# Bound rows through the accumulator, and two kinds of scaling moved to GpSimd, in a two-layer attention and feed-forward kernel

## The chip, the core and the metric

The kernel runs on one core of a Trainium2 chip. The core has five engines with queues of their own: TensorE (PE; its weight loads are shown as PEld), VectorE (DVE), ScalarE (ACT), GpSimd (POOL) and SyncE (SP), which here only issues DMAs. Each engine works through its instructions in the order in which the program was written, and they meet at semaphores. The metric is the device time of one execution in microseconds.

## The reference

The input `A_x` has 2048 tokens of 512 values. Two kinds of layer alternate, A, B, A, B; each adds to its input. A is attention with 32 heads of 16 values and no mask, B is a feed-forward net with 1376 hidden values:

```python
qkv = (layernorm(x) @ wqkv)                      # 32 heads of 16
p = softmax(q @ k^T * 16 ** -0.5)                # 2048 x 2048 for each head
x = x + (p @ v) @ wo
x = x + gelu(layernorm(layernorm(x)) @ w1 + b1) @ w2 + b2
```

Layers 1 and 3 in the kernel's names are the two pairs of A and B. Inputs and output are bfloat16.

## The kernel before, in words

**Segments and tiles.** Attention works in segments: one head group of four heads (`hg`, eight of them), and one unit of queries (512 tokens; the last unit of layer 3 is split into two of 256). A segment has 64 score tiles of 128 keys by 512 queries (16 key blocks times four heads); its scores are transposed, keys on partitions. The first unit of each layer is cut in two parts by keys (`nparts == 2`), since part of the keys is not there yet: in layer 1, key blocks 0 to 3 and then 4 to 15, in layer 3, 0 to 11 and then 12 to 15. So there are 88 segments: 16 in parts and 24 whole ones in layer 1, 16 in parts, 16 whole ones and 16 of half width in layer 3.

**Exponentials without a maximum.** Each head has 32 columns in the stored queries and keys: 16 values, and in column 16 a 1 on the key's side and a bound on the query's side, minus the norm of the query; `scl` multiplies it by the largest norm among the keys of the part. So the score product itself subtracts a bound that no score exceeds. The two key parts of a segment have different bounds; when their sums are merged, the first part is multiplied by the exponential of the difference of the two bounds, which `job_segend` reads from row 16 of each head's 32 rows of the scaled query `QT`.

**Two engines take exponentials.** ScalarE turns groups of two or three score tiles in PSUM into bfloat16 with `Exp` (L1374). For key blocks 3, 6, 9, 12 and 15 (`DK`, 20 of a segment's 64 tiles) VectorE may do it instead: L1466 turns a score into the bits of a bfloat16 that approximates its exponential, and L1497 makes three shifted copies. The four are multiplied by four versions of the values (V and three scaled ones, `vs`, made on GpSimd by L1157 and for whole segments read back from memory). So a tile on VectorE needs four products with the values (L1563), one on ScalarE needs one.

**Accumulation.** L1563 accumulates the products in bank 6 of PSUM (`ACCB`), 17 rows in each of four column tiles: 16 values, and the sum of the weights by a column of ones. At a segment's end `job_segend` transposes the bank to `accT` (L1593). Segments in parts also transpose their `QT` into a slot of `xn` (L1602) and take from it row 16: part 0 keeps it as `rowA` (L1608), part 1 takes the difference (L1618), ScalarE its exponential (L1620), and four instructions on GpSimd merge the parts (L1621 to L1624). Then the sums are divided out (L1626, L1635).

**Queries.** `flow_q` brings a segment's queries by a transposing DMA to one of two slots of `qraw`. `job_qt` waits for one of three slots of `QT` and for `scl`, and scales them (L1132). The slot of `QT` is given back in `job_segend`, after the transposes.

**Normalisation.** `ln_group` makes mean and variance (L846, L847) and, on GpSimd, the reciprocal deviation (L854, L855). `ln_apply` (L859) applies them to one tile of 128 tokens in a slot of `xn`, three in number. `job_qkv_tile` does that ahead of the projections to queries, keys and values (in layer 1 twice for tiles 4 to 15, first for keys and values, later for queries; in layer 3 once), `job_yt` ahead of the feed-forward net. A transposing DMA on SP follows (L893, L1696). The first four tiles of layer 1 have a way of their own (`job_first_tile`), and the last 256 tokens another (`tail_tile`).

**The order of the work.** A planner in the program (`Sched`) simulates the five engines with a duration for each instruction and writes each engine's queue in the order of the simulated time, by priority among what is ready. `take_d` gives a tile to VectorE when its simulated queue is short enough and a bank and a buffer are free; everything else goes to ScalarE. A duration, an instruction or a slot that changes can thus change the order of all the rest. In a second pass (`refill`) it puts products with zeros (L1295, L1297, L1299) into gaps of TensorE. The fields of `I(...)` are the function, the resources read and written, the planner's duration, and two more; `"fast"` marks VectorE instructions that the planner lengthens, by the last field of a GpSimd instruction, where both run at once.

Of the kernel before, what the change touches and what calls it, by code (L numbers as in the profile page):

```python
# [8 lines left out]
BF16 = mybir.dt.bfloat16  # L9
# [5 lines left out]
ALU = mybir.AluOpType  # L15
# [252 lines left out]
def I(fn, reads=(), writes=(), dur=0.3, same_ok=(), lat=None):  # L268
    return (fn, tuple(reads), tuple(writes), tuple(same_ok), dur, lat)
# [231 lines left out]
ACCB = 6  # L501
# [10 lines left out]
class Builder:  # L512
# [45 lines left out]
    def alloc(self, es):  # L558
        nc = self.nc
        S, NT, NC, NFC = self.S, self.NT, self.NC, self.NFC  # L560
        t = lambda name, shape, dt: es.enter_context(nc.sbuf_tensor(name, shape, dt))
# [13 lines left out]
        self.sel = t("sel", [32, 128], BF16)  # L575
        self.onesm = t("onesm", [128, 1], F32)
# [107 lines left out]
    def build_startup(self):  # L684
# [46 lines left out]
        def consts():  # L731
# [10 lines left out]
            yield dve(lambda e: e.tensor_copy(out=self.sel[:, :].rearrange("p (h c) -> p h c", c=32)[:, :, 16], in_=self.m4[:, :]), [("m4",)], [("sel",)])  # L742
            self.S_.mark(("consts",))
# [113 lines left out]
    def ln_apply(self, tt, slot, i, dst, dres, prio):  # L857
        c = 4 * slot + i
        return Task("dve", prio, [I(lambda e: e.tensor_scalar(out=dst, in0=self.xres[:, tt, :], scalar1=self.mv[:, c, 0:1], scalar2=self.rs[:, c:c + 1], op0=ALU.subtract, op1=ALU.mult),  # L859
                                    [("x", tt), ("mv", c), ("rs", slot)], [dres], 0.395, (), "fast")])  # L860
# [21 lines left out]
    def job_qkv_tile(self, L, tt, slot, i, left, prio, what):  # L882
        S_ = self.S_
# [3 lines left out]
        yield self.ln_apply(tt, slot, i, xnr, RX, prio)  # L887
# [236 lines left out]
    def job_qt(self, sg, s):  # L1124
        L, part, hg = sg["L"], sg["part"], sg["hg"]
        k = (L // 2) * 2 + part
        q = yield ("get", "qt")
        sg["qslot"] = q
        yield ("keys", [("scl", L, part)])
        W = sg["W"]  # L1130
        src, RS = (self.psbf(self.q0bank)[:, 0:512], ("ps", self.q0bank)) if s is None else (self.qraw[:, s, 0:W], ("qraw", s))
        yield Task("dve", 0.4, [I(lambda e: e.tensor_scalar(out=self.QT[:, q, 0:W], in0=src, scalar1=self.scl[:, k, hg:hg + 1], scalar2=self.qbias[:, 0:1], op0=ALU.mult, op1=ALU.add),  # L1132
                                  [RS, ("scl", k), ("qbias",)], [("qt", q)], 0.16 + 0.24 * W / 512, (), "fast")])
# [380 lines left out]
    def try_pv(self):  # L1514
        S_ = self.S_
        while True:
# [35 lines left out]
            for (s_, j, res, ap, use, sh) in pick:  # L1552
# [3 lines left out]
                sg["first"].add(hp)  # L1556
                for i, kb in enumerate(kbs):
# [28 lines left out]
    def job_segend(self, sg):  # L1586
# [11 lines left out]
        if nparts == 2:  # L1598
            xs = yield ("get", "xn")
            RX = ("xn", xs)  # L1600
            rowT = self.xn[:, xs, :].rearrange("p (b r) -> p b r", r=32)
            yield Task("dve", 1.2, [I(lambda e: e.transpose(self.xn[:, xs, :], self.QT[:, q, :]), [("qt", q)], [RX], 0.68)])  # L1602
# [4 lines left out]
        if nparts == 2 and part == 0:  # L1607
            yield Task("dve", 1.2, [I(lambda e: e.tensor_copy(out=self.rowA[:, hg, :], in_=rowT[:, :, 16]), [RX], [("rowA", hg)], 0.17)])  # L1608
            S_.release("xn", xs)
# [5 lines left out]
        if nparts == 2:  # L1615
            dw = self.dw[:, hg % 2, :]
            RW = ("dw", hg % 2)
            yield Task("dve", 1.2, [I(lambda e: e.tensor_tensor(out=dw, in0=rowT[:, :, 16], in1=self.rowA[:, hg, :], op=ALU.subtract), [RX, ("rowA", hg)], [RW], 0.17)])  # L1618
            S_.release("xn", xs)
# [69 lines left out]
    def job_yt(self, L, tt, slot, i, left, pr):  # L1689
        S_ = self.S_  # L1690
        xr = yield ("get", "xn")
        yield self.ln_apply(tt, slot, i, self.xn[:, xr, :], ("xn", xr), pr - 1)
# [237 lines left out]
```

## Time and profile before

| what | value |
|---|---|
| median of 3 runs | 1602.69 us (1601.01 to 1605.23) |
| profiled execution | 1603.4 us, its span 1601.8 us |
| busy, VectorE | 1473.8 us (92%) |
| busy, ScalarE | 1535.5 us (96%) |
| busy, GpSimd | 207.0 us (13%) |
| L1602, L1132, L859 on VectorE | 32, 88 and 74 instructions |
| segments' ends (L1593) | 88, from 33.9 to 1578.4 us |

Engines are named PE, PEld, DVE, ACT, POOL and SP in the profile; `L1374` is line 1374 of the kernel. A group's row has the line, the engine, the operation, what it writes and reads, the shapes and the count; then busy time in us and the mean of one in ns; then the idle time of its engine just before it, and what ended it. A row of stages has the stretch in us, its length, the busy time and number of instructions for each engine, the granted clock of PE, the busy share of the DMA engines and their GB/s. A row of a timeline has start and duration in us, and in brackets the idle time before and what ended it.

### The profile page before, as it was taken

To read this page: it belongs to the slowest core of one execution; us is meant where nothing else is said; L and a number is where in the kernel's file an instruction comes from. 1 tells how busy PE (TensorE), PEld (TensorE's weight loads), DVE (VectorE), ACT (ScalarE), POOL (GpSimd) and SP (SyncE) were. 2 spreads that over 40 slices of the span, in tenths; PEclk is the share of its full clock that TensorE was granted. 3 is DMA by queue.
4 is the path that set the end of the run, shared out by engine and by line. 5 is a ranking of instruction groups with operands and counts; after the bars stand their busy time and mean duration, and the time that the engine had idled before them with its cause. 6 is when DMAs were issued, how large, how long until landed. Compare 5 with 4: busy or idle time off the path is not lost.

```text
span 1601.8 us, 39236 instructions
## 1 busy us (share of the span) xinstructions
PE 1571.1 (98%) x16532; PEld 481.3 (30%) x16532; DVE 1473.8 (92%) x3323; ACT 1535.5 (96%) x1366; POOL 207.0 (13%) x406
## 2 busy tenths in 40 slices
PE   9999999999999999999999999999999999999998
PEld 3222222222222222222222233222222222344454
DVE  7999999999999899989999899999899989998893
ACT  6999999999999999989999989999999999999995
POOL 4464210000200001001211124300000000000000
PEclk9999999999999999999999999999999999999999
DMA  6671011213321122222822232210101100211100
GB/s 168 122 168 63 22 31 31 53 30 76 84 44 46 36 62 80 56 61 77 138 45 64 58 71 67 60 26 21 31 15 37 31 22 18 40 40 40 41 22 20
DMA packets 212464, 88.79 MB, mean 55 GB/s; under 512 B 183835, under 2 KB 206656, under 8 KB 212288
## 3 DMA queue, kind: packets, MB, share of 16 engines
q1 hardware_dynamic: 212288, 86.29, 24.0%
q8 instruction: 129, 2.11, 0.6%
q14 instruction: 47, 0.39, 0.1%
HBM read 34.65 MB, written 19.48 MB: 34 GB/s over the span
## 4 chain that ended last, share of the span: by engine, by line
PE 49%; ACT 28%; DVE 20%; issue 1%; DMA 1%; POOL 1%; POOLq 0%; DVEq 0%
ACT PT L1374 25%; PE ps L1389 17%; PE ps L1563 14%; DVE dp L1466 7%; DVE dp L1497 5%; PE ps L1747 4%; PE ps L1704 4%; PE ps L916 4%; PE ps L1295 3%; ACT h L1739 2%; PE ps L1299 1%; DVE accT L1593 1%; PE ps L1297 1%; DVE st L846 1%; PE ps L1649 1%
## 5 line engine op out<-in xcount | busy, mean ns | idle before, releaser
L1374 ACT ACTIVATE PT<-ps 128x1024 bf16<-128x1024 f32 (+1 forms) x1283 | 1457.1, 1269 | 36.0 <-PE ps L1389 30.1
L1389 PE MATMUL ps<-QT,KT 32*128 32x512 bf16 (+1 forms) x4608 | 672.5, 358 | 11.5 <-DVE dp L1466 2.2
L1466 DVE TENSOR_SCALAR dp<-ps 128x512 uint16<-128x512 f32 x921 | 618.7, 683 | 56.7 <-PE ps L1389 54.0
L1497 DVE TENSOR_SCALAR dp<-dp 128x1024 uint16<-128x1024 uint16 (+1 forms) x1410 | 533.0, 421 | 7.4 <-PE ps L1563 3.3
L1563 PE MATMUL ps<-PT,V 128*17 128x512 bf16 (+1 forms) x3568 | 468.3, 358 | 0.0
L1563 PE MATMUL ps<-dp,vs 128*17 128x512 bf16 (+1 forms) x3120 | 441.0, 357 | 0.7 <-DVE dp L1497 0.6
L1389 PEld LDWEIGHTS ps<-QT,KT 32*128 32x128 bf16 x4608 | 169.9, 91 | 541.8 <-ACT PT L1374 260.4
L1563 PE MATMUL ps<-dp,V 128*17 128x512 bf16 (+1 forms) x1040 | 214.5, 357 | 2.3 <-DVE accT L1593 2.0
L1297 PE MATMUL ps<-zw 32*128 32x444 bf16 (+2 forms) x714 | 197.6, 325 | 0.0
L1563 PEld LDWEIGHTS ps<-dp,vs 128*17 128x17 bf16 x3120 | 110.9, 88 | 125.1 <-issue 100.9
L1563 PEld LDWEIGHTS ps<-PT,V 128*17 128x17 bf16 x3568 | 112.3, 88 | 105.3 <-issue 94.4
L1299 PE MATMUL ps<-zw 128*32 128x448 bf16 (+23 forms) x1621 | 142.6, 318 | 0.7 <-DVE dp L1466 0.6
L1295 PE MATMUL ps<-zw 128*128 128x448 bf16 (+17 forms) x560 | 130.6, 334 | 4.1 <-DVE dp L1466 2.2
L854 POOL TENSOR_SCALAR rs<-mv 128x4 f32<-128x4 f32 (+2 forms) x19 | 6.6, 347 | 879.1 <-DVE mv L847 877.7
L1704 PE MATMUL ps<-yT,wf 128*128 128x512 bf16 (+3 forms) x396 | 103.5, 360 | 1.0 <-DVE yT L1830 0.5
L916 PE MATMUL ps<-wqkv,xnT 128*128 128x512 bf16 x336 | 93.1, 382 | 1.0 <-DVE h L929 0.5
L1157 POOL TENSOR_SCALAR vs<-V 128x340 bf16<-128x340 bf16 (+2 forms) x72 | 60.5, 841 | 139.7 <-PE ps L1563 121.6
L1295 PEld LDWEIGHTS ps<-zw 128*128 128x128 bf16 x560 | 42.9, 98 | 83.5 <-issue 52.7
L1563 PEld LDWEIGHTS ps<-dp,V 128*17 128x17 bf16 x1040 | 51.3, 88 | 53.1 <-issue 28.5
L1728 DVE TENSOR_SCALAR h<-ps,b1c 128x512 bf16<-128x512 f32 (+2 forms) x88 | 62.3, 708 | 1.8 <-PE ps L1704 1.5
L1593 DVE STREAM_TRANSPOSE accT<-ps 128x512 f32<-128x512 f32 (+1 forms) x88 | 58.1, 660 | 6.1 <-PE ps L1563 4.9
L1299 PEld LDWEIGHTS ps<-zw 128*32 128x32 bf16 x1621 | 52.4, 95 | 24.7 <-DVE dp L1466 5.7
(172 smaller groups left out, 903.0 us busy)
## 6 DMA issues: line engine op xcount, KB each, us to landing
vs<-vs_scr SPq DMA_DIRECT2D x56, 255.0 KB, 2.7
wf<-in_B_w_dram SPq DMA_DIRECT2D x90, 128.0 KB, 2.8
q_scr<-qk SPq DMA_DIRECT2D x22, 256.0 KB, 2.4
k_scr<-qk SPq DMA_DIRECT2D x12, 256.0 KB, 2.3
out_dram<-xres SPq DMA_DIRECT2D x16, 128.0 KB, 1.7
vs_scr<-vs SPq DMA_DIRECT2D x8, 255.0 KB, 3.8
xres<-in_A_x_dram SPq DMA_DIRECT2D x7, 256.0 KB, 3.1
v_scr<-vst SPq DMA_DIRECT2D x12, 136.0 KB, 1.8
```

Of the source, the lines that this page charges most:

```text
L916: yield Task("pe", prio, [I(lambda e, c=c: e.matmul(self.ps[:, b, :], lhsT=xnT[:, c, :], rhs=self.wqkv[:, c, which * 512:which * 512 + 512 ...
L1295: fn = lambda e: e.matmul(self.ps[:, b, 0:w], lhsT=self.zw[:, 0:128], rhs=self.zw[:, 0:w], start=st, stop=st, skip_group_check=True)
L1297: fn = lambda e: e.matmul(self.ps[:, b, 0:w], lhsT=self.zw[32 * p:32 * p + 32, 0:128], rhs=self.zw[32 * p:32 * p + 32, 0:w], start=st, sto ...
L1299: fn = lambda e: e.matmul(self.ps[32 * p:32 * p + 32, b, 0:w], lhsT=self.zw[:, 0:32], rhs=self.zw[:, 0:w], start=st, stop=st, skip_group_c ...
L1374: S_.submit(Task("act", 1e-5 * gi, [I(lambda e, pt=pt, n=n, b0=b0: e.activation(out=self.PT[:, pt:pt + n, :], in_=self.ps[:, b0:b0 + n, :] ...
L1389: return [I(lambda e, kb=kb, i=i: e.matmul(self.ps[:, b, i * W:(i + 1) * W], lhsT=self.KT[32 * hp:32 * hp + 32, hg, kb * 128:(kb + 1) * 12 ...
L1466: self.S_.submit(Task("dve", 0.0, [I(lambda e: e.tensor_scalar(out=self.dp[:, u, w * 512:(w + 1) * 512], in0=self.ps[:, b, :], scalar1=BIT ...
L1497: yield Task("dve", pr, [I(lambda e, k=k, v=v: e.tensor_scalar(out=self.dp[:, v, 0:N], in0=self.dp[:, u, 0:N], scalar1=float(SHIFT[k]), sc ...
L1563: ops.append((nth[j, sh] + 0.1 * i, I(lambda e, hp=hp, v=v, ap=ap[:, i * W:(i + 1) * W], first=first and i == 0, W=W: e.matmul(self.ps[32 ...
L1593: yield Task("dve", 0.3, [I(lambda e: e.transpose(self.accT[:, a, 0:W], self.ps[:, ACCB, 0:W]), [("ps", ACCB)], [RA], 0.17 + 0.535 * W / 5 ...
L1704: yield Task("pe", pr, [I(lambda e, c=c: e.matmul(self.ps[0:M, b, off:off + W], lhsT=self.w1(fc, c), rhs=self.yT[:, c, 0:W], start=(c == 0 ...
L1747: yield Task("pe", pr, [I(lambda e, fc=fc, i=i, b=b: e.matmul(self.ps[:, b, :], lhsT=self.gt(fc, i, W), rhs=self.w2(L, fc), start=(fc == 0 ...
```

## The change

A new constant `rsel` has, for each head of a group, a matrix of 128 x 18 with a single 1: it picks row 16 of the head's 32 rows of `QT` and puts it into row 17 of the head's column tile. For segments in parts, this product opens the accumulation of each head, so the bound row lies beside the sums in `accT` after the transpose, and `QT` is not transposed any more. `rowA` and the difference are read from `accT`. `job_qt` uses GpSimd from the fifth segment on. `ln_apply` uses GpSimd in `job_qkv_tile` for tiles 0 to 11, and in `job_yt` for all but the last four tiles of layer 1. The planner's durations for both on GpSimd are 1.49 us at full width.

```diff
+        self.rsel = t("rsel", [128, 4, 18], BF16)
...
+            yield dve(lambda e: e.memset(self.rsel[:, :, :], 0.0), [], [("rsel",)], 0.1)
+            yield dve(lambda e: e.tensor_copy(out=self.rsel[:, :, 17], in_=self.iogt[:, :]), [("iogt",)], [("rsel",)], 0.1)
...
-    def ln_apply(self, tt, slot, i, dst, dres, prio):
+    def ln_apply(self, tt, slot, i, dst, dres, prio, eng="dve"):
...
-        return Task("dve", prio, [...
-                                    [("x", tt), ("mv", c), ("rs", slot)], [dres], 0.395, (), "fast")])
+        return Task(eng, prio, [...
+                                    [("x", tt), ("mv", c), ("rs", slot)], [dres], 0.395 if eng == "dve" else 1.49, (), "fast" if eng == "dve" else 0.09)])
...
-        yield self.ln_apply(tt, slot, i, xnr, RX, prio)
+        yield self.ln_apply(tt, slot, i, xnr, RX, prio, "dve" if tt >= 12 else "pool")
...
-        yield Task("dve", 0.4, [...
-                                  [RS, ("scl", k), ("qbias",)], [("qt", q)], 0.16 + 0.24 * W / 512, (), "fast")])
+        eng = "dve" if sg["i"] < 4 else "pool"
+        yield Task(eng, 0.4, [...
+                                  [RS, ("scl", k), ("qbias",)], [("qt", q)], 0.16 + 0.24 * W / 512 if eng == "dve" else 0.21 + 1.28 * W / 512, (), "fast" if eng == "dve" else 0.09)])
...
+                if first and sg["nparts"] == 2:
+                    first = False
+                    ops.append((nth[j, sh] - 0.1, I(lambda e, hp=hp, q=q: e.matmul(self.ps[32 * hp:32 * hp + 18, ACCB, :], lhsT=self.rsel[:, hp, :], rhs=self.QT[:, q, :], start=True, stop=False, skip_group_check=True, tile_position=(0, 32 * hp)),
+                                                     [("rsel",), ("qt", q)], [("ps", ACCB)], W / 2400.0, [("ps", ACCB)], ("col", hp))))
...
-        if nparts == 2:
-            xs = yield ("get", "xn")
-            RX = ("xn", xs)
-            rowT = self.xn[:, xs, :].rearrange("p (b r) -> p b r", r=32)
-            yield Task("dve", 1.2, [I(lambda e: e.transpose(self.xn[:, xs, :], self.QT[:, q, :]), [("qt", q)], [RX], 0.68)])
...
-            yield Task("dve", 1.2, [I(lambda e: e.tensor_copy(out=self.rowA[:, hg, :], in_=rowT[:, :, 16]), [RX], [("rowA", hg)], 0.17)])
-            S_.release("xn", xs)
+            yield Task("dve", 1.2, [I(lambda e: e.tensor_copy(out=self.rowA[:, hg, :], in_=T[:, :, 17]), [RA], [("rowA", hg)], 0.17)])
...
-            yield Task("dve", 1.2, [I(lambda e: e.tensor_tensor(out=dw, in0=rowT[:, :, 16], in1=self.rowA[:, hg, :], op=ALU.subtract), [RX, ("rowA", hg)], [RW], 0.17)])
-            S_.release("xn", xs)
+            yield Task("dve", 1.2, [I(lambda e: e.tensor_tensor(out=dw, in0=T[:, :, 17], in1=self.rowA[:, hg, :], op=ALU.subtract), [RA, ("rowA", hg)], [RW], 0.17)])
...
-        yield self.ln_apply(tt, slot, i, self.xn[:, xr, :], ("xn", xr), pr - 1)
+        yield self.ln_apply(tt, slot, i, self.xn[:, xr, :], ("xn", xr), pr - 1, "dve" if L == 1 and tt >= 12 else "pool")
```

More of the change, by code (lines that the diff above doesn't have):

```diff
@@ L855, in ln_group @@
         yield Task("pool", prio, [I(lambda e: e.tensor_tensor(out=rs, in0=rs, in1=self.cneg[:, 0:n], op=ALU.pow), [R, ("cneg",)], [R], 0.45 + 0.15 * n)])
-    def ln_apply(self, tt, slot, i, dst, dres, prio):
+    def ln_apply(self, tt, slot, i, dst, dres, prio, eng="dve"):
         c = 4 * slot + i
-        return Task("dve", prio, [I(lambda e: e.tensor_scalar(out=dst, in0=self.xres[:, tt, :], scalar1=self.mv[:, c, 0:1], scalar2=self.rs[:, c:c + 1], op0=ALU.subtract, op1=ALU.mult),
-                                    [("x", tt), ("mv", c), ("rs", slot)], [dres], 0.395, (), "fast")])
+        return Task(eng, prio, [I(lambda e: e.tensor_scalar(out=dst, in0=self.xres[:, tt, :], scalar1=self.mv[:, c, 0:1], scalar2=self.rs[:, c:c + 1], op0=ALU.subtract, op1=ALU.mult),
+                                    [("x", tt), ("mv", c), ("rs", slot)], [dres], 0.395 if eng == "dve" else 1.49, (), "fast" if eng == "dve" else 0.09)])
     def dma(self, fn, reads, writes, prio, dur=0.08, lat=None):
@@ L1131, in job_qt @@
         src, RS = (self.psbf(self.q0bank)[:, 0:512], ("ps", self.q0bank)) if s is None else (self.qraw[:, s, 0:W], ("qraw", s))
-        yield Task("dve", 0.4, [I(lambda e: e.tensor_scalar(out=self.QT[:, q, 0:W], in0=src, scalar1=self.scl[:, k, hg:hg + 1], scalar2=self.qbias[:, 0:1], op0=ALU.mult, op1=ALU.add),
-                                  [RS, ("scl", k), ("qbias",)], [("qt", q)], 0.16 + 0.24 * W / 512, (), "fast")])
+        eng = "dve" if sg["i"] < 4 else "pool"
+        yield Task(eng, 0.4, [I(lambda e: e.tensor_scalar(out=self.QT[:, q, 0:W], in0=src, scalar1=self.scl[:, k, hg:hg + 1], scalar2=self.qbias[:, 0:1], op0=ALU.mult, op1=ALU.add),
+                                  [RS, ("scl", k), ("qbias",)], [("qt", q)], 0.16 + 0.24 * W / 512 if eng == "dve" else 0.21 + 1.28 * W / 512, (), "fast" if eng == "dve" else 0.09)])
         if s is None:
```

## The prediction

> **What bounds the kernel now.** I read the page's busy times and chain first, then its groups, then busy time by stage, last the instructions around one stage boundary. The lines of the page:
>
> ```profile
> PE 1571.1 (98%) x16532; PEld 481.3 (30%) x16532; DVE 1473.8 (92%) x3323; ACT 1535.5 (96%) x1366; POOL 207.0 (13%) x406
> ...
> PE 49%; ACT 28%; DVE 20%; issue 1%; DMA 1%; POOL 1%; POOLq 0%; DVEq 0%
> ...
> L1374 ACT ACTIVATE PT<-ps 128x1024 bf16<-128x1024 f32 (+1 forms) x1283 | 1457.1, 1269 | 36.0 <-PE ps L1389 30.1
> ...
> L1466 DVE TENSOR_SCALAR dp<-ps 128x512 uint16<-128x512 f32 x921 | 618.7, 683 | 56.7 <-PE ps L1389 54.0
> L1497 DVE TENSOR_SCALAR dp<-dp 128x1024 uint16<-128x1024 uint16 (+1 forms) x1410 | 533.0, 421 | 7.4 <-PE ps L1563 3.3
> ```
>
> ScalarE takes exponentials by L1374 and waits 30 us for scores in the whole run; VectorE takes the rest by L1466 and three L1497. PE's 98% is no bound: L1295, L1297 and L1299 multiply zeros. Of 4096 score tiles (8 head groups x 4 heads x 16 key blocks x 4 query units x 2 layers), 921 go to VectorE at (618.7 + 533.0) / 921 = 1.251 us each, 3175 to ScalarE at 1457.1 / 3175 = 0.459. So the end is set by how the two share tiles. With both full, f us taken off VectorE move f / (1.251 + 0.459) tiles, worth 0.459 / 1.710 = 0.268 f. With ScalarE alone the bound and VectorE tiles to be had, it would be 0.459 / 1.251 = 0.367 f; where none are to be had, nothing.
>
> Busy time by stage; columns are PE, PEld, DVE, ACT, POOL:
>
> ```profile
> 33.90:92.90 59.00, 57.76 (x391) 16.67 (x391) 53.84 (x108) 54.70 (x58) 26.70 (x40) 1.00 0.62 116
> 92.90:234.00 141.10, 137.30 (x1440) 39.94 (x1440) 138.04 (x311) 138.69 (x129) 50.52 (x106) 1.00 0.28 68
> 234.00:421.10 187.10, 185.97 (x1798) 49.24 (x1798) 176.49 (x399) 185.88 (x162) 9.44 (x18) 1.00 0.22 52
> ...
> 809.50:958.30 148.80, 147.36 (x1356) 41.47 (x1359) 139.67 (x309) 143.12 (x122) 24.76 (x48) 1.00 0.28 59
> 958.30:1019.50 61.20, 59.20 (x617) 19.40 (x608) 59.25 (x135) 54.23 (x54) 30.20 (x60) 1.00 0.31 74
> 1019.50:1200.50 181.00, 178.80 (x1804) 47.12 (x1804) 171.14 (x388) 179.12 (x156) 5.76 (x8) 1.00 0.12 27
> ```
>
> From 92.9 to 234 both are full (idle 3.1 and 2.4 us). In 234 to 421 ScalarE idles 1.2 us, VectorE 10.6: there the 20 tiles of 64 that VectorE may take in a segment run out while the long gelu holds ScalarE. From 958.3, ScalarE idles 7.0 us: a wait. The boundary of layer 3's two key parts, from the engines' timelines:
>
> ```profile
> 962.04 0.23 DVE L1102 TENSOR_SCALAR scl<-ps,onesm 128x8 f32<-128x8 f32 x1 [0.51 <-PE ps L1101]
> 962.37 0.89 DVE L1132 TENSOR_SCALAR QT<-qraw,scl,qbias 128x512 bf16<-128x512 bf16 x2
> ...
> 963.60 12.75 ACT L1374 ACTIVATE PT<-ps 128x1536 bf16<-128x1536 f32 x11 [6.03 <-PE ps L1389]
> ...
> 961.59 5.37 POOL L1157 TENSOR_SCALAR vs<-V 128x136 bf16<-128x136 bf16 x9
> ```
>
> ScalarE waits 6.03 us for scores that wait for L1132, and that for L1102.
>
> **The Trainium skill.** "SBUF — State Buffer", "Who interferes with whom": a VectorE instruction in a two-port mode and a GpSimd instruction exclude each other, and the loser blocks fully. The trace agrees in kind, not in degree: of 1353 wide L1497, 1184 meet no GpSimd instruction and average 0.419 us, 169 meet one and average 0.477, the longest 0.962; an L992 of otherwise 0.26 us took 1.36 under four L1497 in a row (954.35). "GPSIMD Engine Reference", "4.1 Engine selection", gives elementwise work to VectorE and bars GpSimd from PSUM. The trace agrees on speed, below; the one L1132 that reads PSUM is among the four that stay. "Perfetto Trace Analysis", "Identifying the Most-Contended Engine", calls PE's busy share no measure of headroom; the zero products here agree.
>
> **The change part by part.** Prices come from groups kept apart by shape:
>
> ```profile
> L1132 DVE TENSOR_SCALAR QT<-qraw,scl,qbias 128x512 bf16<-128x512 bf16 x71 | 28.7, 406 | 0.4
> L859 DVE TENSOR_SCALAR xn<-xres,mv,rs 128x512 bf16<-128x512 bf16 x70 | 27.7, 428 | 3.8 <-POOL rs L855 2.8 <-DMA xnT<-xn 0.3 <-DMA yT<-xn 0.2
> L1157 POOL TENSOR_SCALAR vs<-V 128x340 bf16<-128x340 bf16 x24 | 26.0, 1084 | 31.2 <-PE ps L1563 30.0
> L1602 DVE STREAM_TRANSPOSE xn<-QT 128x512 bf16<-128x512 bf16 x32 | 22.0, 686 | 0.7 <-DMA xnT<-xn 0.7
> L1157 POOL TENSOR_SCALAR vs<-V 128x136 bf16<-128x136 bf16 x24 | 14.8, 619 | 6.1 <-PE ps L1299 5.1
> ```
>
> VectorE loses 32 transposes L1602 (22.0 us), 84 scalings L1132 (68 x 0.404 + 16 of half width at 0.313 = 32.5) and 54 of 70 applications L859 (54 x 27.7/70 = 21.4): 75.9 us. The 32 small copies and differences now read accT and stay.
>
> GpSimd gains 138 instructions. From L1157, (1084 - 619) / 204 = 2.28 ns an element puts 512 elements at 1084 + 172 x 2.28 = 1476 ns and 256 at 892: 122 x 1.476 + 16 x 0.892 = 194 us, so 207 become 401. L1157 has one operation and these have two; at 32 elements L994 with two takes 298 ns. Bounds: 1.2 to 2.5 us; I take 1.476.
>
> Contention: 169 x 0.058 = 9.8 us for 207 us of GpSimd, 0.047 a us, so 0.069 for one moved instruction and 9 us for all. Bounds: none, to 0.4 an instruction (55 us).
>
> PE gains 128 picking products, four side by side, 32 turns. Sixteen L1563 take 0.97 us in the chain, so a turn is 0.24 and all are 7.8 us. Zero products hide them: between 92.9 and 234 L1295, L1297 and L1299 show 20.3, 25.8 and 20.2 us. Without that cover, 7.8 us. QT is long there when the accumulation starts, and the query buffer comes free at the accumulator's transpose, earlier than now (first: 33.9 and 38.3). The two start-up instructions that make the picking matrix cost 0.11 and 0.17 by their nearest rows (L741, L742), before a 0.80 us wait of VectorE at 9.4: nothing.
>
> Moved steps and their queues: L859 on GpSimd ends 1.07 us later, and its DMA transpose on SP follows. Among layer 1's key tiles the smallest gap from L859 to that DMA is 2.1 us (57.7 to 59.8), 1.7 after the old duration: covered. The DMA that refills qraw waits 1.07 longer on SP, with a segment of slack; uncovered, it costs that much each. From 80 to 120 GpSimd has 26.9 us; 8 applications and 4 scalings add 17.7, making 44.6 in 40. What queues there is L1157 (shifted values) and L992 to L996 (bound rows of later queries); the next 40 us have 17.5 + 3.0 and clear it. I take nothing, with 4.6 us as the other end.
>
> The sum, f being what leaves VectorE less contention:
> - 33.9 to 92.9: ScalarE bound, no VectorE tiles: 0.
> - 92.9 to 234: L1602 5.5, L1132 3.8, one L859 0.4, less 0.6: 9.1 x 0.268 = 2.4.
> - 234 to 809.5: 9.2 + 8.9, less 3.3: 14.8. VectorE idles 37.8 us there, so I count six tenths: 2.4.
> - 809.5 to 958.3: its end hangs on layer 1's last feed-forward and keys, to L1102 at 962: 0.
> - 958.3 to 1019.5: 5.5 + 4.1 - 0.7 = 8.8, 2.4 saved; L1132 behind L1102 is on the path and takes 1.48 for 0.40: -1.1. Net 1.3.
> - 1019.5 to 1578.4: 10.4 + 5.2 - 2.6 = 13.1 at six tenths: 2.1.
>
> Together 8.2 us: the span of 1601.8 becomes 1593.6. The profiled execution took 1603.4 and the median is 1602.69, so the time is 1594.5.
>
> **The rivals.** (1) More gain: the earlier query buffer and empty transposition slots help the planner as well, and contention is near nothing: 76 x 0.367 = 28 at most, some 20 likely, 1582. For it: VectorE has no idle time in a third of the segments. Against: tiles run out in others.
>
> (2) No change: the planner gives every instruction another place, the tiles still run out where the gelu lies, and 4.6 + 1.1 us go to queues: 1602. For it: VectorE's 37.8 and 45.1 us of idle time in the two long stretches.
>
> (3) Slower: the scaled queries come late in the short segments after 958.3, which last 4 to 8 us. For each, GpSimd has three L1157 (1.86), four merge instructions (0.66 + 0.35 + 0.26 + 0.74 = 2.0), and now 1.48: 5.3 us. A scaling behind both others ends 5 us later than now. Three buffers give one to two segments of lead. If 2.3 us of each remain uncovered, 8 x 2.3 = 18, less 6.9 gained elsewhere, gives 1614; above 1.5 us uncovered the kernel is slower by over 0.3%. Against: the buffer is free earlier, and 30.2 + 11.8 of 61.2 us is no full queue.
>
> **How the numbers follow.** What a measurement of this kernel can tell from no change is about 0.3%, 4.8 us. Forecast 0.45 (its own range 1586 to 1598), more gain 0.10, no change 0.20, slower 0.25. So faster 0.55, same 0.20, slower 0.25. The range of 1582 to 1612 leaves out half of the more-gain case and the upper part of the slower one.
>
> **What would show it.** Right: VectorE tiles rise from 921 to about 950 (67 / 1.710 = 39 at full use, some 30 with the factors above); GpSimd busy near 400 us, its new groups near 1.48 us; L1497 below 0.44 mean; ScalarE's wait near 962 longer by one to three us. Wrong: tiles not above 930, ScalarE waiting more than 50 us for L1389, GpSimd groups of 2 us, or L1497 above 0.46.

## The result and the profile after

The changed kernel takes 1620.62 us (median of 5 runs, 1618.09 to 1622.89) against 1602.69: 1.0109 of the time before, interval 1.0094 to 1.0125, or 17.9 us more. I had forecast 1594.5, with 0.55 on faster; the range of 1582 to 1612 does not hold it. Its profiled execution took 1618.1 us, its span 1616.3.

Busy times, the chain and the groups of the page after, in the order of those of before, and last the two groups that are new on GpSimd (the scalings at full width, from the view that keeps shapes apart; 16 of half width take 649 ns each):

```profile
PE 1546.2 (96%) x16212; PEld 475.6 (29%) x16349; DVE 1455.6 (90%) x3184; ACT 1531.0 (95%) x1359; POOL 392.3 (24%) x544
...
PE 52%; DVE 22%; ACT 19%; POOL 4%; issue 3%; DMA 1%; SPq 0%; POOLq 0%; DVEq 0%
...
L1378 ACT ACTIVATE PT<-ps 128x1536 bf16<-128x1536 f32 (+1 forms) x1276 | 1452.3, 1263 | 59.9 <-PE ps L1393 53.4
...
L1470 DVE TENSOR_SCALAR dp<-ps 128x512 uint16<-128x512 f32 x938 | 628.1, 681 | 63.9 <-PE ps L1393 60.8
L1501 DVE TENSOR_SCALAR dp<-dp 128x1024 uint16<-128x1024 uint16 (+1 forms) x1422 | 559.8, 435 | 13.0 <-PE ps L1571 7.7
...
L862 POOL TENSOR_SCALAR xn<-xres,mv,rs 128x512 bf16<-128x512 bf16 x54 | 124.9, 2321 | 1.3
L1136 POOL TENSOR_SCALAR QT<-qraw,scl,qbias 128x512 bf16<-128x512 bf16 x68 | 60.3, 887 | 610.3 <-PE ps L1393 607.5 <-DVE scl L1105 2.5 <-DMA qraw<-q_scr 0.3
```

(L1378 is L1374 of before, L1470 is L1466, L1501 is L1497, L1393 the score product L1389, L1571 the product with the values L1563, L862 the application L859, L1136 the scaling L1132, L1705 the first feed-forward product L1704.) VectorE did take tiles over, 938 for 921, and ScalarE has 4.5 us less to do. But both now stand: ScalarE waits 53.4 us for scores (30.1 before), VectorE is idle 160.7 us of its span (128.0 before). The kernel is longer because its two workers wait, not because they have more to do. And an application costs 2321 ns on GpSimd, where I had 1476 and the planner 1490.

By stage (columns PE, PEld, DVE, ACT, POOL), cut at the same segment ends as before:

```profile
95.00:240.70 145.70, 137.52 (x1408) 38.90 (x1411) 140.95 (x308) 140.48 (x130) 70.88 (x124) 1.00 0.27 69
240.70:432.90 192.20, 185.30 (x1732) 49.81 (x1750) 176.66 (x385) 187.31 (x162) 35.30 (x34) 0.99 0.21 49
...
821.30:976.30 155.00, 149.25 (x1373) 42.70 (x1389) 137.88 (x303) 143.37 (x123) 34.57 (x66) 1.00 0.31 66
976.30:1026.60 50.30, 47.84 (x560) 14.21 (x553) 49.68 (x111) 48.81 (x49) 36.16 (x59) 1.00 0.27 57
1026.60:1212.90 186.30, 180.69 (x1829) 50.29 (x1847) 173.51 (x381) 183.21 (x159) 20.18 (x19) 1.00 0.14 28
```

Against before these are 145.7 for 141.1 us, 192.2 for 187.1, 155.0 for 148.8, 50.3 for 61.2, and 186.3 for 181.0. Of the 14.5 us by which the span is longer, 11.7 are lost before 432.9, where 24 of the 54 applications on GpSimd lie. From 432.9 to 821.3, with 16 more of them, it is as long as before (388.5 for 388.4), so the loss does not simply follow their number. Nor is each stage to be read alone, since work moves across the cuts: 821.3 to 976.3 has no application on GpSimd, and the stage of 50.3 us, where my rival (3) saw scaled queries come late, takes 136 score tiles for 154. The last three stages shown take 391.6 us together, for 391.0. ScalarE idles 1.5 us in the stage of 50.3.

What a wait looks like, from the engines' timelines around 290 us:

```profile
283.31 4.21 POOL L862 TENSOR_SCALAR xn<-xres,mv,rs 128x512 bf16<-128x512 bf16 x2
287.50 1.09 POOL L1136 TENSOR_SCALAR QT<-qraw,scl,qbias 128x512 bf16<-128x512 bf16 x1
288.58 4.90 POOL L862 TENSOR_SCALAR xn<-xres,mv,rs 128x512 bf16<-128x512 bf16 x2
...
290.68 4.01 SPq L1697 DMA_TRANSPOSE yT<-xn  x2
...
297.76 0.38 PE L1705 MATMUL ps<-yT,wf 128*128 128x512 bf16 x1 [1.63 <-DVE dp L1501]
...
298.58 1.02 ACT L1378 ACTIVATE PT<-ps 128x1024 bf16<-128x1024 f32 x1 [1.17 <-PE ps L1393]
```

GpSimd needs 10.2 us for four applications and a scaling; by the planner's prices it is 7.5. The last transposing DMA goes out at 293.50, when the last application is done, and lands at 297.30. TensorE, whose queue is in order, stands 1.63 us at the feed-forward product that reads it, with the next scores behind. (The profile names an L1501 as the releaser, since one ended at 297.68. But the weights of this product are the transposed tile, and their load stood until 297.51, just after the landing.) ScalarE then waits 1.17 us for those scores.

### The profile page after: what moved, and what is told of

It is laid out like the page before. It is cut to its first block, busy times and chain, and to the rows that moved or that the text cites. A ratio compares the mean times of both kernels' runs of the same rounds, so it can differ in the third digit from the quotient of the medians.

```text
span 1616.3 us, 38841 instructions
## 1 busy us (share of the span) xinstructions
PE 1546.2 (96%) x16212; PEld 475.6 (29%) x16349; DVE 1455.6 (90%) x3184; ACT 1531.0 (95%) x1359; POOL 392.3 (24%) x544
## 4 chain that ended last, share of the span: by engine, by line
PE 52%; DVE 22%; ACT 19%; POOL 4%; issue 3%; DMA 1%; SPq 0%; POOLq 0%; DVEq 0%
PE ps L1393 18%; ACT PT L1378 17%; PE ps L1571 15%; DVE dp L1470 9%; DVE dp L1501 6%; PE ps L1748 4%; PE ps L1705 4%; PE ps L1299 3%; PE ps L919 3%; POOL xn L862 2%; PE ps L1650 2%; DVE accT L1601 1%; ACT h L1740 1%; PE ps L1301 1%; PE ps L1303 1%
## 5 line engine op out<-in xcount | busy, mean ns | idle before, releaser
L1378 ACT ACTIVATE PT<-ps 128x1536 bf16<-128x1536 f32 (+1 forms) x1276 | 1452.3, 1263 | 59.9 <-PE ps L1393 53.4
L1393 PE MATMUL ps<-QT,KT 32*128 32x512 bf16 (+1 forms) x4608 | 678.4, 359 | 17.5 <-DVE dp L1470 5.7
L1470 DVE TENSOR_SCALAR dp<-ps 128x512 uint16<-128x512 f32 x938 | 628.1, 681 | 63.9 <-PE ps L1393 60.8
L1501 DVE TENSOR_SCALAR dp<-dp 128x1024 uint16<-128x1024 uint16 (+1 forms) x1422 | 559.8, 435 | 13.0 <-PE ps L1571 7.7
L1571 PE MATMUL ps<-PT,V 128*17 128x512 bf16 (+1 forms) x3550 | 475.3, 359 | 0.3 <-issue 0.3
L1571 PE MATMUL ps<-dp,vs 128*17 128x512 bf16 (+1 forms) x3174 | 447.7, 358 | 0.6 <-DVE dp L1501 0.5
L1393 PEld LDWEIGHTS ps<-QT,KT 32*128 32x128 bf16 x4608 | 170.7, 91 | 554.9 <-ACT PT L1378 252.8
L1136 POOL TENSOR_SCALAR QT<-qraw,scl,qbias 128x512 bf16<-128x512 bf16 (+1 forms) x84 | 70.7, 841 | 791.0 <-PE ps L1393 788.2
L1571 PE MATMUL ps<-dp,V 128*17 128x512 bf16 (+1 forms) x1058 | 212.9, 358 | 2.3 <-DVE dp L1470 1.1
L1301 PE MATMUL ps<-zw 32*128 32x444 bf16 (+6 forms) x716 | 198.7, 325 | 0.0
L1571 PEld LDWEIGHTS ps<-dp,vs 128*17 128x17 bf16 x3174 | 111.6, 88 | 126.8 <-issue 102.7
L1571 PEld LDWEIGHTS ps<-PT,V 128*17 128x17 bf16 x3550 | 113.8, 88 | 102.8 <-issue 91.1
L862 POOL TENSOR_SCALAR xn<-xres,mv,rs 128x512 bf16<-128x512 bf16 x54 | 124.9, 2321 | 1.3
L1299 PE MATMUL ps<-zw 128*128 128x448 bf16 (+16 forms) x502 | 120.2, 335 | 4.2 <-DVE dp L1470 1.9
L1303 PE MATMUL ps<-zw 128*32 128x448 bf16 (+22 forms) x1312 | 122.0, 323 | 0.5 <-DVE dp L1470 0.4
L1705 PE MATMUL ps<-yT,wf 128*128 128x512 bf16 (+3 forms) x355 | 93.1, 358 | 16.2 <-DMA yT<-xn 5.7
L1571 PEld LDWEIGHTS ps<-dp,V 128*17 128x17 bf16 x1058 | 52.3, 88 | 47.7 <-issue 28.4
L1299 PEld LDWEIGHTS ps<-zw 128*128 128x128 bf16 x502 | 38.8, 98 | 75.9 <-issue 45.5
## 6 DMA issues: line engine op xcount, KB each, us to landing
wf<-in_B_w_dram SPq DMA_DIRECT2D x90, 128.0 KB, 2.9
out_dram<-xres SPq DMA_DIRECT2D x16, 128.0 KB, 1.7
```

The lines of the kernel that those rows point to most:

```text
L862: return Task(eng, prio, [I(lambda e: e.tensor_scalar(out=dst, in0=self.xres[:, tt, :], scalar1=self.mv[:, c, 0:1], scalar2=self.rs[:, c:c ...
L1299: fn = lambda e: e.matmul(self.ps[:, b, 0:w], lhsT=self.zw[:, 0:128], rhs=self.zw[:, 0:w], start=st, stop=st, skip_group_check=True)
L1301: fn = lambda e: e.matmul(self.ps[:, b, 0:w], lhsT=self.zw[32 * p:32 * p + 32, 0:128], rhs=self.zw[32 * p:32 * p + 32, 0:w], start=st, sto ...
L1303: fn = lambda e: e.matmul(self.ps[32 * p:32 * p + 32, b, 0:w], lhsT=self.zw[:, 0:32], rhs=self.zw[:, 0:w], start=st, stop=st, skip_group_c ...
L1378: S_.submit(Task("act", 1e-5 * gi, [I(lambda e, pt=pt, n=n, b0=b0: e.activation(out=self.PT[:, pt:pt + n, :], in_=self.ps[:, b0:b0 + n, :] ...
L1393: return [I(lambda e, kb=kb, i=i: e.matmul(self.ps[:, b, i * W:(i + 1) * W], lhsT=self.KT[32 * hp:32 * hp + 32, hg, kb * 128:(kb + 1) * 12 ...
```

## The experiments

Four theories. **A, the price:** the queues are written in advance with the planner's durations, 1.49 us for both moved operations; where the chip takes longer, what is queued behind stands. **B, replanning:** any edit reorders everything, and this order is a poor one. **C, contention:** GpSimd slows VectorE's copies by more than I counted. **D, the clock:** TensorE's granted clock halves in places, and that is the loss. A gives a time that falls as the price of the application nears 2.3 us, whatever else is in the kernel; B gives none in particular; C gives the same time for the same GpSimd work, whatever the price; D gives one that falls with more zero products. All kernels here compute the whole reference. "Before" is 1602.4 to 1602.7 us beside each of them.

### The parts of the change alone

The picking product alone (the changed kernel with both moves undone), the scalings alone and the applications alone (on the kernel before), and the change without its applications:

```diff
 pick alone
-        yield self.ln_apply(tt, slot, i, xnr, RX, prio, "dve" if tt >= 12 else "pool")
+        yield self.ln_apply(tt, slot, i, xnr, RX, prio)
-        eng = "dve" if sg["i"] < 4 else "pool"
+        eng = "dve"
-        yield self.ln_apply(tt, slot, i, self.xn[:, xr, :], ("xn", xr), pr - 1, "dve" if L == 1 and tt >= 12 else "pool")
+        yield self.ln_apply(tt, slot, i, self.xn[:, xr, :], ("xn", xr), pr - 1)
```

> The kernel before with the picking product alone: 32 transposes of QT gone from VectorE, 128 products more on TensorE, nothing more on GpSimd. Theory A: 1593 to 1600 us, a little faster, since nothing is reckoned wrongly; VectorE's tiles 921 to 930. If the loss lies in the picking product (TensorE's turn before each accumulation): 1604 to 1612.

1597.56 us, 0.9973 (0.9964 to 0.9983). ScalarE waits 30.4 us, as before.

> The kernel before with the query scalings on GpSimd alone, the planner told 1.49 us as in the change. If that wrong price hurts by itself: 1607 to 1615 us. If it hurts only in a particular order: 1600 to 1605.

The scalings alone, at the planner's 1.49: 1603.14 us, 1.0004 (0.9995 to 1.0013).

> The kernel before with the 54 layer-norm applications on GpSimd and nothing else. Theory A: as slow as the whole change or slower, 1616 to 1626 us, the application near 2.3 us, ScalarE's wait for scores 45 to 60 us. Theory B: anywhere between 1605 and 1620. Theory C: 1606 to 1612.

The applications alone, at 1.49: 1622.32 us, 1.0124 (1.0106 to 1.0141). This one part gives the whole loss, without the picking product and without a scaling on GpSimd.

> The change without its second half: picking product and query scalings on GpSimd, all layer-norm applications back on VectorE. Theory A (the applications on GpSimd take 2.3 us where the planner reckons 1.49, so the queues written for 1.49 stand still on TensorE and ScalarE): the loss is gone and some of the forecast gain is left, 1592 to 1600 us, ScalarE's wait for scores back near 30 us. Theory B (replanning alone costs: any new order of the queues is worse than the old one): still slower, 1610 to 1620. Theory C (GpSimd's traffic lengthens VectorE's copies; half of that traffic is left): 1606 to 1612, L1501's mean above 430 ns.

Picking product and scalings without the applications: 1612.9 us, 1.0058 (1.0043 to 1.0073). This I had not expected, since both parts alone cost nothing. Its profile shows one place of 13.7 us at half the clock, taken up below.

### The price of the application, on the kernel before

Only the planner's number changes; the chip does the same work (54 applications of 2.3 us on GpSimd, no picking product, scalings on VectorE).

```diff
 applications alone, three more prices: 1.90, 2.25, 3.00
-    [("x", tt), ("mv", c), ("rs", slot)], [dres], 0.395 if eng == "dve" else 1.49, (), "fast" if eng == "dve" else 0.09)])
+    [("x", tt), ("mv", c), ("rs", slot)], [dres], 0.395 if eng == "dve" else 2.25, (), "fast" if eng == "dve" else 0.09)])
```

> The kernel before with the applications on GpSimd, subtract and multiply, the planner told 2.25 us. With 1.49 this took 1622.3. Theory A: the wrong price was the loss, 1601 to 1608 us. If the length of the application on GpSimd is the loss (keys and the feed-forward net start later whatever the order): 1614 to 1622.

> The kernel before with the applications on GpSimd, the planner told 1.90 us (2.3 was measured; 1.49 gave 1622.3 and 2.25 gave 1604.4). Theory A, the distance of the price from the truth on the short side: between the two, 1607 to 1617 us. Theory B, luck of the order: anything from 1603 to 1622, with no relation to the price.

> The same, the planner told 3.00 us, 0.7 us too long. Theory A: too long makes no engine wait in an unplanned place, so 1602 to 1609 us. If any wrong price costs, short or long: 1612 to 1622. Theory B: anything in that range.

| planner's price | 1.49 | 1.90 | 2.25 | 3.00 |
|---|---|---|---|---|
| time, us | 1622.32 | 1617.92 | 1604.36 | 1603.18 |
| ratio to before | 1.0124 | 1.0097 | 1.0013 | 1.0010 |
| ScalarE waits for scores, us | 49.2 | 42.9 | 32.9 | 31.6 |
| mean granted clock of the runs | 0.988-0.994 | 0.995-0.998 | 0.998-1.000 | 0.998-1.000 |

The time falls at each step until the price reaches the duration that the trace shows (2280 to 2343 ns in these runs), and then stays. Four orders of the same work stand in line with A; chance orders (B) would do so only by luck, one time in 24, and C would leave them equal. Too short a price costs 18 us, one that is too long nothing. In the chain of waits, the feed-forward product waits for its DMA at 1.49 and not at 2.25. First the kernel with 1.49, then the one with 2.25 (columns: us in total, times, longest):

```profile
ACT PT L1374 <- PE ps L1389: 49.2, 92, 4.0
PE ps L1704 <- DMA yT<-xn: 6.1, 3, 2.8
```

```profile
ACT PT L1374 <- PE ps L1389: 32.9, 79, 3.1
```

### The price in the whole change

```diff
 applications priced
-    [dres], 0.395 if eng == "dve" else 1.49, (), "fast" if eng == "dve" else 0.09)])
+    [dres], 0.395 if eng == "dve" else 2.25, (), "fast" if eng == "dve" else 0.09)])
 both priced, besides
-    0.16 + 0.24 * W / 512 if eng == "dve" else 0.21 + 1.28 * W / 512, (), "fast" if eng == "dve" else 0.09)])
+    0.16 + 0.24 * W / 512 if eng == "dve" else 0.35 + 0.45 * W / 512, (), "fast" if eng == "dve" else 0.09)])
```

> The whole change, with the planner told that a layer-norm application on GpSimd takes 2.25 us instead of 1.49. The chip's work is the same. Theory A: the queues fit what happens, so most of the loss is gone: 1596 to 1606 us, TensorE's waits for yT and ScalarE's 53 us for scores back near 30. Theory B and theory C: no better than the change, 1614 to 1624. If the applications hurt by their length itself (the feed-forward and key chains start later), 1610 to 1618.

> The whole change, with the planner told 2.25 us for an application on GpSimd (1.49 in the change) and 0.80 us for a full scaling (1.49 in the change; 0.89 was measured). Theory A: the scaling was reckoned too long, which makes nobody wait, so about what the application's price alone gave, 1603 to 1610 us. If queues written for a scaling that is too long cost as well (buffers given back later than they could be, SP's order), 1596 to 1603.

Applications priced: 1608.09 us, 1.0033 (1.0020 to 1.0046), so 12.5 of the 17.9 us. Both priced: 1603.82, 1.0010 (1.0004 to 1.0017), another 4.3. What the chip has to do on GpSimd is unchanged, and about two thirds of what the waits for scores had grown are gone (53.4 us in the changed kernel, 38.2 here, 30.1 before), as the page of this kernel shows, and then the waits of the changed kernel and of this one:

```profile
PE 1564.9 (98%) x16549; PEld 476.0 (30%) x16549; DVE 1457.5 (91%) x3194; ACT 1531.0 (96%) x1359; POOL 394.8 (25%) x544
...
L862 POOL TENSOR_SCALAR xn<-xres,mv,rs 128x512 bf16<-128x512 bf16 x54 | 124.5, 2313 | 1.0
```

```profile
PE ps L1705 <- DMA yT<-xn: 5.7, 3, 2.6
```

```profile
ACT PT L1378 <- PE ps L1393: 38.2, 96, 2.7
PE ps L1705 <- DMA yT<-xn: 1.3, 1, 1.3
```

GpSimd 394.8 for 392.3, VectorE 1457.5 for 1455.6, ScalarE 1531.0 for 1531.0: the same work 17 us faster.

### The operation itself

The application subtracts the mean and multiplies; the scaling, on the same shape and types, multiplies and adds, and takes 887 ns. So I wrote the application as x r + (-mean r), and then, to keep one operation of the pair, as x r - mean r. `nb` is made on GpSimd by two small instructions for a group of tiles, in the second form by one.

```diff
 multiply, add
+    e.tensor_tensor(out=nb, in0=mean, in1=rs, op=ALU.mult)
+    e.tensor_scalar(out=nb, in0=nb, scalar1=-1.0, scalar2=0.0, op0=ALU.mult, op1=ALU.add)
...
+    e.tensor_scalar(out=dst, in0=self.xres[:, tt, :], scalar1=self.rs[:, c:c + 1], scalar2=self.nb[:, c:c + 1], op0=ALU.mult, op1=ALU.add), ..., 0.85, (), 0.09
 multiply, subtract (against multiply, add)
-    e.tensor_scalar(out=nb, in0=nb, scalar1=-1.0, scalar2=0.0, op0=ALU.mult, op1=ALU.add)
...
-    op0=ALU.mult, op1=ALU.add)
+    op0=ALU.mult, op1=ALU.subtract)
```

> The whole change, with the application on GpSimd written as x * r + (-mean * r), multiply and add with two pointers like the query scaling, in place of subtract and multiply; two small instructions a group make -mean * r; the planner reckons 0.85 us. If the pair of operations makes the price, the application takes 0.75 to 0.9 us like the query scaling (0.887) and theory A expects 1586 to 1598 us. If the source or the destination makes it, the application stays at 2.1 to 2.4 us and theory A expects 1620 to 1640. Theory B: 1605 to 1620.

> The whole change, with the norm applied on GpSimd as x * r - mean * r (multiply, subtract), so that one of the pair of operations of the changed kernel is kept, the other not. If subtract is what makes the GpSimd application dear, its group reads about 2.2 us, GpSimd's queue stands as in the changed kernel (the planner has 0.85) and the time is 1615 or above. If it is the order or the pair subtract-then-multiply alone, the group reads 0.77 to 0.95 us, as with multiply and add, and the time lies with that one, 1598 to 1606. A value between leaves both.

Multiply, add: 1601.68 us, 0.9996 (0.9986 to 1.0006). Multiply, subtract: 1642.56 us, 1.0249 (1.0233 to 1.0264). The groups of the application on GpSimd (duration of one in ns: least, median, most), of the changed kernel, then with multiply and add, then with multiply and subtract:

```profile
L862 POOL TENSOR_SCALAR xn<-xres,mv,rs x54: 2069/2200/3025, 26.8 to 1513.4; 128x512 bf16<-128x512 bf16 x54
```

```profile
L868 POOL TENSOR_SCALAR xn<-xres,rs,nb x54: 767/777/1467, 28.8 to 1494.9; 128x512 bf16<-128x512 bf16 x54
```

```profile
L867 POOL TENSOR_SCALAR xn<-xres,rs,nb x54: 2069/2234/2842, 27.3 to 1562.9; 128x512 bf16<-128x512 bf16 x54
```

The subtraction alone makes the price: 2069 ns at least in either place, 767 without it. And the last kernel is the sharpest look at theory A. Its GpSimd work (401.8 us) is nearly that of the changed kernel, but the planner has 0.85 for what takes 2.28, and it loses 40.1 us. With the scalings' price left at 1.49, the whole change with 0.85, 1.49 and 2.25 for an application of 2.3 us takes 1642.6, 1620.6 and 1608.1. One place of it, in the timelines of GpSimd, SP, TensorE and ScalarE:

```profile
1267.60 9.34 POOL L867 TENSOR_SCALAR xn<-xres,rs,nb 128x512 bf16<-128x512 bf16 x4
1276.93 0.77 POOL L1143 TENSOR_SCALAR QT<-qraw,scl,qbias 128x512 bf16<-128x512 bf16 x1
...
1269.79 8.36 SPq L1704 DMA_TRANSPOSE yT<-xn  x4
...
1280.00 1.48 PE L1712 MATMUL ps<-yT,wf 128*128 128x512 bf16 x3 [2.04 <-DMA yT<-xn]
1281.42 1.03 PE L1400 MATMUL ps<-QT,KT 32*128 32x512 bf16 x4
...
1282.07 1.45 ACT L1385 ACTIVATE PT<-ps 128x1536 bf16<-128x1536 f32 x1 [2.78 <-PE ps L1400]
```

This is the mechanism: the applications end late, the fourth transpose goes out late, TensorE stands 2.04 us at the feed-forward product, the scores (L1400) lie behind it in its queue, and ScalarE waits 2.78 us for them. One part is still to come. From 1278.2 on TensorE's granted clock is halved for 13.7 us, and ScalarE goes on idling with no GpSimd instruction and no DMA left to wait for (the third column from the end is the clock):

```profile
1284.50:1292.00 7.50, 7.17 (x44) 0.97 (x44) 3.53 (x9) 4.45 (x4) 0.00 (x0) 0.51 0.00 1
```

> The whole change with the application as multiply and add, the planner told 0.85 us for it and 0.80 for a full scaling; all prices then near what the chip takes. Theory A: 1592 to 1599 us, faster than the kernel before by 0.2 to 0.6%; VectorE's tiles 940 to 950. If the moves themselves have no value beside GpSimd's contention: 1599 to 1604.

> The whole change, norms as x * r + (-mean * r) with the planner's price at their measured mean (0.93) and the query scalings at 1.10 as in the best kernel so far. If what GpSimd takes over is eaten by contention, it does no better than the kernel without the norms: 1595 to 1600. If the norms were a gain once cheap and well priced, 1588 to 1593. If a price at the mean is not enough (some take 1.5 us), 1600 to 1606.

Multiply and add with the scalings priced at 0.80: 1601.88 us, 1.0007 (0.9994 to 1.0021). With the application at 0.93 and the scalings at 1.10: 1605.02, 1.0017 (1.0010 to 1.0025). Four orders of the whole change in which no price is far too short thus lie within 3.3 us, 1601.7 to 1605.0. Differences of that size between orders I ascribe to nothing, and the 4.3 us of the scalings' price above are hardly more. But 3.3 us is no bound: the order without applications, whose one wrong price is too long, took 1612.9. So the 12.5 us alone would not rule out a chance order. The row of four prices, the 40 us and the waits in the traces speak for A.

### The clock

> The whole change, and the planner's second pass aims at 0.65 of TensorE's time in each 3.4 us window instead of 0.55, so more zero products stand in the planned gaps; the order of all other work is the same. Theory D (a gap that was not planned leaves a window of TensorE too empty, the granted clock halves for 3.4 us or more, and that costs more than the gap): fewer stretches at half clock, 1608 to 1616 us. Theory A (the stalls themselves are the loss): 1617 to 1624, since a full TensorE queue waits as long for yT.

> The change with the application on GpSimd as multiply and add, and the zero products aimed at 0.65 as in the run beside it. Theory D: no stretch at half clock, 1594 to 1599 us, faster than the kernel before by 0.2 to 0.5%. Without theory D: 1600 to 1604, as with 0.55.

More zero products (`FILL_U = 0.55` to `0.65`) in the changed kernel: 1622.62 us, 1.0129 (1.0112 to 1.0146), no gain, and ScalarE waits 56.6 us. In the kernel with multiply and add: 1600.11, 0.9985 (0.9979 to 0.9992). More zeros are thus no cure. But they did not test D, since they did not take the halved clock away: its stretches add up to 13.6 us in the changed kernel with more zeros and to 10.2 without. In the changed kernel they come after waits (from 294.8 us, the place shown above):

```profile
294.80:298.20 3.40, 1.54 (x11) 0.42 (x9) 2.88 (x7) 2.26 (x2) 0.00 (x0) 1.00 0.48 34
298.20:301.60 3.40, 3.40 (x24) 0.48 (x22) 1.49 (x4) 2.48 (x2) 0.00 (x0) 0.51 0.00 0
```

The changed kernel has three such stretches of 3.4 us, the kernel with multiply and subtract seven, 47.7 us in all, the picking product alone one of 10.2, "applications priced" one of 13.7, the kernels before and "both priced" none (the last 3 us of a kernel left out).

What the halved clock costs can be read from runs of one kernel that differ in it. The kernel with the picking product and the scalings at 1.49 took 1606.57 us in the run whose mean clock was 1.000, and 1616.07 and 1617.77 in the two with 0.993. A mean of 0.993 over 1617 us is 22.6 us at half the clock (2 x 0.007 x 1617), and the runs are 9.5 and 11.2 us longer: nearly half of such time is lost. The kernel with multiply and add and both prices has the same, 1599.79 to 1602.20 at 1.000, and 1613.93 at 0.992. By this, as an estimate, the changed kernel (0.994 to 0.997, 0.996 on average) owes some 5 to 8 of its 17.9 us to the clock, and the one with multiply and subtract (0.984 to 0.985) 20 to 25 of its 40. In the rows above the clock comes back to 1.000 as the price comes right. "Applications priced" took 1604.57 and 1604.86 in its two runs at 1.000, so most of the 4.3 us between it and "both priced" is clock too. D is thus no rival to A but a part of the loss. In the places shown the wait comes first; no run took the halved clock away and left the waits.

### The price of the scalings

With the picking product and without applications on GpSimd, the scalings were given four prices; on the chip they take 0.86 to 0.92 us at full width.

```diff
 three more prices at full width: 0.60, 0.80, 1.10
-    0.16 + 0.24 * W / 512 if eng == "dve" else 0.21 + 1.28 * W / 512, (), "fast" if eng == "dve" else 0.09)])
+    0.16 + 0.24 * W / 512 if eng == "dve" else 0.35 + 0.75 * W / 512, (), "fast" if eng == "dve" else 0.09)])
```

> Picking product and query scalings on GpSimd, layer-norm applications on VectorE, the planner told 0.80 us for a full scaling instead of 1.49. With 1.49 this took 1612.9. If the wrong price of the scaling made that loss: 1594 to 1601 us. If the scaling on GpSimd costs by its place (the queries' DMAs on SP wait for it, VectorE's copies lengthen): 1606 to 1613.

> Picking product and query scalings on GpSimd, applications on VectorE, the planner told 1.10 us for a full scaling (0.86 to 0.92 was measured; 1.49 gave 1612.9 and 0.80 gave 1598.0). If a price that is too long costs by its distance: 1600 to 1607 us. If the 1612.9 was the order of one place: 1595 to 1600.

> The same, the planner told 0.60 us for a full scaling, 0.3 us too short. Theory A: scalings that come later than reckoned make scores wait, 1602 to 1610 us, unless the two buffers ahead cover it; then 1596 to 1600.

| planner's price | 0.60 | 0.80 | 1.10 | 1.49 |
|---|---|---|---|---|
| time, us | 1603.41 | 1597.99 | 1595.57 | 1612.9 |
| ratio to before | 1.0009 | 0.9970 | 0.9958 | 1.0058 |
| ScalarE waits for scores, us | 36.5 | 32.4 | 29.3 | 40.5 |
| mean granted clock of the runs | 0.998-1.000 | 1.000 | 1.000 | 0.993-1.000 |

At 0.60, well below the duration, the time rises by 5.4 us, as A has it, though by little more than orders differ. The point at 1.49 does not fit: too long a price is free in the two other tests of it (3.00 for the applications, 1.49 for the scalings alone). In the profile of that kernel, TensorE waits 1.63 us at a feed-forward product and then runs at half its clock for 13.7 us, in which ScalarE is busy 6.91:

```profile
1425.90:1429.30 3.40, 1.77 (x38) 1.01 (x35) 2.90 (x7) 3.29 (x3) 0.23 (x1) 1.00 0.40 65
1429.30:1443.00 13.70, 13.37 (x140) 4.96 (x140) 7.66 (x18) 6.91 (x6) 0.00 (x0) 0.50 0.09 21
```

This kernel is 15 us slower than the one at 0.80, but only 8.6 in its run at a clock of 1.000 (1606.57). Why this order has the place, and where those 8.6 us lie, stays open.

The kernel at 1.10 is the fastest of all: 1595.57 us, 0.9958 of before (0.9943 to 0.9973), 6.9 us less, with the picking product and the scalings on GpSimd and the applications left on VectorE.

### Contention, read from the traces

Wide copies (L1497, L1501 and their like) are about 0.416 us where they meet no GpSimd instruction. What those that meet one take more:

| kernel | GpSimd busy, us | copies that meet it | mean of these, us | in all, us |
|---|---|---|---|---|
| before | 207.0 | 169 of 1353 | 0.477 | 9.8 |
| pick alone | 202.1 | 176 of 1374 | 0.475 | 10.4 |
| pick and scalings (1.10) | 270.7 | 251 of 1383 | 0.479 | 15.8 |
| multiply, add | 328.3 | 314 of 1386 | 0.481 | 20.7 |
| both priced | 394.8 | 379 of 1386 | 0.499 | 32.2 |
| changed kernel | 392.3 | 351 of 1392 | 0.502 | 29.8 |

So the move costs VectorE 20 us in its copies alone. C is a true term, but not the loss: the changed kernel and "both priced" have the same of it and lie 17 us apart. "SBUF — State Buffer", "Who interferes with whom", in the Trainium skill has the loser blocked for the whole of the other's instruction. The traces agree for one GpSimd instruction and not for the moved ones. Of 17 copies of the changed kernel that meet the merge L1625 (0.76 us), 12 take over 0.6 us, up to 0.957, and each of the 12 ends 0.28 us after L1625 does. But of 111 copies that begin during an application, 2.3 us long, none takes more than 0.876, also where it begins early: none is held through the whole of it.

## Why the prediction was wrong, point by point

**The step that failed: the prices of the moved work, and what a wrong price does.** I took 1.476 us for the 122 instructions of full width (0.892 for the 16 others) and added "L859 on GpSimd ends 1.07 us later ... covered". Measured: 2.321 us for an application, 0.887 for a scaling at full width, 0.649 at half. The sum, 195.6 us for my 194, is right by accident; GpSimd's total "near 400" came true and told nothing. My bounds of 1.2 to 2.5 held the 2.3. But I used them only for GpSimd's load, not for the order: I never set the planner's 1.49 beside a measured duration and asked what stands behind an instruction that takes 0.8 us longer than its queue was written for. Where the cover "2.1 us" seemed enough for one application, there come two, three or four in a row (6.20 us for three at 80.7, 9.34 for four above), and the delay adds up over them. My row, L1157, was a multiplication; the operation I priced with it subtracts.

That error makes 12.5 us of the loss in the whole change, and 18 to 19 in the applications alone. Part of it comes by way of TensorE's clock, which the prediction put at nothing: by the estimate above some 5 to 8 us of the whole loss.

**GpSimd between 80 and 120.** I took nothing, "4.6 us as the other end". There three applications of 6.20 us stand ahead of the small instruction (L1101) from which the key norm and `scl` follow. VectorE has its input ready at 83.7, stands 3.6 us until L1101 is done, and ScalarE waits 2.54 us at 89.8 and 2.20 at 94.2 (before, 2.2 us in all from 80 to 120). The timelines, and VectorE's wait from the list of waits:

```profile
80.66 6.20 POOL L862 TENSOR_SCALAR xn<-xres,mv,rs 128x512 bf16<-128x512 bf16 x3
86.83 0.56 POOL L1101 TENSOR_TENSOR kmx<-kmx,chalf 32x1 f32<-32x1 f32 x1
...
89.79 1.03 ACT L1378 ACTIVATE PT<-ps 128x1024 bf16<-128x1024 f32 x1 [2.54 <-PE ps L1393]
94.22 5.97 ACT L1378 ACTIVATE PT<-ps 128x1536 bf16<-128x1536 f32 x5 [2.20 <-PE ps L1393]
...
DVE krhs L1102 <- POOL kmx L1101: 4.3, 2, 3.6
```

I had listed L1157 and L992 to L996 as what queues there, not L1098 (now L1101), on which the start of the second key part hangs.

**Contention.** "9 us for all" was 20: the 0.069 us of a moved instruction were 0.145. The size was off by two, within my bound of 55. It is not all: with prices that fit, the moves are still worth nothing. The picking product alone takes 1597.56 us, "both priced" 1603.82. Of the 53 us of VectorE instructions that the moves take away, its copies take 22 back. With the rest it takes 16 tiles more (939 for 923), and ScalarE has 3.7 us less to do (1531.0 for 1534.7), but stands 7.8 us longer for scores (38.2 for 30.4). What makes it stand there is not shown.

**Tiles.** Forecast some 950, measured 938. The groups that left VectorE carried some 75 us (forecast 75.9), right; but its copies take 26.8 us more, 20 of them contention, and its idle time grew by 32.7.

**The picking product.** The one part that did what I said. Hidden on TensorE, it takes 32 transposes from VectorE, and gives 5 us (1602.5 to 1597.6). My own factors have for the transposes (5.5 + 5.5) x 0.268, 2.9 us; the rest is within what orders differ by.

**The boundary near 962.** Right in kind, small in size. ScalarE's wait there is 6.49 us for 6.03, where I had one to three more; two scalings on GpSimd take 1.53 us.

```profile
971.67 0.23 DVE L1105 TENSOR_SCALAR scl<-ps,onesm 128x8 f32<-128x8 f32 x1 [0.34 <-PE ps L1104]
972.00 1.53 POOL L1136 TENSOR_SCALAR QT<-qraw,scl,qbias 128x512 bf16<-128x512 bf16 x2
973.93 7.03 ACT L1378 ACTIVATE PT<-ps 128x1536 bf16<-128x1536 f32 x6 [6.49 <-PE ps L1393]
```

**The rivals.** (3) had the sign and two thirds of the size (1614), but the wrong instruction and the wrong place: what came late were applications and what stood behind them, the bound of layer 1's keys and the tiles of the feed-forward net, not queries in the short segments. (2), no change, is what the change would have been with prices that fit. Of the signs that I gave for being wrong, two came: GpSimd groups of 2 us and ScalarE waiting over 50 us.

## What to carry to other kernels

Where queues are written from a table of durations, an operation moved to another engine needs a price measured there, for its own pair of operations and not for a like shape. A price too short makes the in-order queues stand: between a quarter and a half of its summed error came out in the time (12.5 us of 54 x 0.83, 40 of 54 x 1.43), a good part of it through TensorE's clock. One too long cost nothing at 3.00 and with the scalings alone, but one order with it was slow for a reason that is not known. Compare the granted clock of runs before you call a wait the whole of a loss. Test a suspected price by changing only the planner's number: the chip's work stays the same, and a row of three or four values tells a price from a chance order. And total busy time is no check of two prices: two errors of opposite sign give the right sum.

## What was not expected of the hardware

On GpSimd, over 128x512 bfloat16 with two per-partition operands, multiply and add take 763 to 767 ns at least in the runs here, and subtract in either place makes it 2062 to 2071. The first agrees with "GPSIMD Engine Reference", "3.1 Elementwise — side-by-side cycle accounting" in the Trainium skill, which has 769 ns for 512 elements in its best case. I could have priced the scalings by it. For the second the measurement stands alone.

TensorE's granted clock falls to 0.50 or 0.51 for stretches of 3.4 us and multiples, without a full window of idleness before: 1.54 us busy of 3.40 at the place above, and 0.81 to 2.71 us before the 27 stretches in the traces of all 20 kernels (first 30 us and last 4 left out). The stretches of a run start on a grid of 3.413 us (in the changed kernel they start 208.21 and 965.97 us apart, 61 and 283 times as much). Of the windows of that grid at full clock, 16 had TensorE busy for less than half, and half the clock followed all 16; of 127 with half to 0.8, it followed 11; of 9004 with more, none. "TensorE: Matmul & The Clock Gate", "What's actually happening", has the half clock and the window of about 3.4 us, but an idle window as the cause; here half-idle ones sufficed.
